# Routing steps at three points of each f-tile, earlier weight requests and a picking mask in halves, in a fused FFT, MLP and capacity-routed MoE kernel

## The chip, the cores and the metric

One core of one Trainium2 chip runs the whole program. The metric is the device time of one execution in microseconds (us). The kernel before took 3361.14 us, the median of three runs from 3357.68 to 3364.51 us.

## The reference, cut to what matters

```python
X = np.fft.fft(np.fft.fft(x, axis=1), axis=2).real      # x: 8 x 3072 x 256
t = X.reshape(24576, 256)
t = (sigmoid(t @ w_gate) * (t @ w_val)) @ w_out         # d_ff 1536
logits = t @ moe2_w_gate                                # 24576 x 8
cap = 24576 // 8                                        # 3072 tokens for each expert
for idx in np.argsort(-logits.flatten()):               # greedy, best pairs first
    tok, e = idx // 8, idx % 8
    if assigned[tok] < 0 and counts[e] < cap:
        assigned[tok] = e; counts[e] += 1
for e in range(8):
    out[assigned == e] = np.maximum(t[assigned == e] @ w1[e], 0) @ w2[e]   # 256 -> 1024 -> 256
```

Every expert ends with exactly 3072 tokens.

## The kernel before, in words

The program has three stages: the transform, the gated MLP, and the routed experts (`Moe2`). The change touches the last alone. There the work goes in eight rounds, one for each expert, in the order in which the experts fill up.

**The experts' matmuls.** A round's 3072 tokens are six token tiles of 512. Each token tile has eight f-tiles (128 of the 1024 hidden columns), so a round has 48 f-tiles. `run` counts them as (c, g) with c from 0 to 11 and g from 0 to 3; two values of c make one token tile. For an f-tile `ffn1` (L1259) issues six matmuls of 512 columns, ScalarE takes the Relu and rounds it (`hh`, L1271), VectorE forms the rest (`hl`, L1272), and `ffn2` (L1275) of the f-tile two places earlier issues twelve matmuls of 256 columns. At the end of a token tile ScalarE copies `y` out and GpSimd (POOL) issues four scatters into `out_dram` (L1293). `xturn` (L1243) transposes the next token tile at g = 2 and 3 of odd c: four transposes on TensorE, `xh` on ScalarE and `xl` on VectorE, with one PSUM buffer for both halves. The expert's weights come by `wload` (L1223), an indirect DMA of POOL, and are split into a high and a low part by `wsplit` (L1232) on ScalarE and VectorE. `gather` (L1211) fetches half a token tile with two indirect DMAs of POOL. POOL executes its queue in the order in which the program issues.

**The routing.** `route(r)` (L1056) finds round r's expert and tokens. If r is above 0 it first takes the best open logit of each token (`best`, eight VectorE instructions over 128x192), marks the winners in V (two VectorE instructions over 128x1536, L1074 and L1076), turns V onto K with twelve transposes in three groups (`turn`, L1020, in PSUM buffers `rt`, of which there are two), and prepares two counts. Then it finds a threshold by 32 bisection steps: two small matmuls onto `cs` (L1095, L1097), two tiny VectorE instructions (`m`, `cand`), a count over one half of K on VectorE (`junk`, L1110) and over the other on ScalarE (`jka`, L1113), whose results the next `cs` matmuls read. Then it finds the expert (`es`, L1121), again takes `best`, scans (L1136), forms the weights' row numbers `wi` (L1140), adds up over partitions with two matmuls on `cs` (L1144, L1145), and writes the ranks RR and RF (L1153 to L1157). The last round has no bisection. `pick(r)` (L1175) turns ranks into token numbers: for each of three h a mask G and a mask H in two halves (VectorE, L1189 and L1192), then four times k two matmuls of H with RF (`rt`, L1201), a small copy on ScalarE (`pc`), two counts on VectorE (`jk`, L1205) and the numbers `idx` (L1207).

**The order.** It is written out when the program is built. `route` and `pick` are generators; each `yield wait, cost` gives the number of beats until the next step and a cost in us. `beat` (L1316) is called once for each f-tile, ahead of `ffn1`. It adds 1.96 us to a budget, less 0.6 for each weight split or transpose of the f-tile, and advances the two streams: the chain of `route` whenever its wait is over, the picks only while the budget is at least 0.2. `want` (L1327) forces steps out at once where a gather or a weight load needs them: the weight loads stand at (10, 1) and (10, 3) of the round before, the next round's first two gathers at (10, 2) and (10, 3), the others 8 f-tiles ahead of their transposes. `chain` (L1298) starts `route(r)` once six of the 24 token columns of round r-1 are picked. Before round 0 all of `route(0)` and the first picks are forced, then four more steps of the chain.

The engines each execute in program order, so a `cs` matmul, a `turn` or a pick's matmul stands in TensorE's queue between the matmuls of the experts, and a count stands in VectorE's queue between the `hl`.

```python
            for c in range(12):
                at = (r, c - 2 - c % 2, c % 2) if c > 1 else (r - 1, 10, 2 + c)
...
                    self.beat(0.6 * len(split))
                    self.ffn1(r, x, 4 * o + g)
                    late.append((r, C, 4 * o + g, self.hid))
                    for p in split:
                        p[0](*p[1:])
                    if len(late) > CFG['lag']:
                        self.ffn2(*late.pop(0))
```

## Time and profile before

| | us |
|---|---|
| median of three runs | 3361.14 |
| the profiled execution, its own time | 3368.34 |
| its span | 3366.6 |
| TensorE matmul busy in the span | 3133.5 (93%) |
| VectorE busy | 2712.7 (81%) |
| ScalarE busy | 1524.2 (45%) |
| POOL busy | 1853.0 (55%) |

The span is 1.7 us shorter than the execution's own time. The stretches of it: the transform to about 418 us, the MLP to about 1994 us, the first routing to 2092 us, then the eight expert rounds, the last of which ends at 3343 us, and the last scatters. Busy time of TensorE counts pipelined matmuls, so that a full engine reads as all of a stretch. An idle time in square brackets is that of the engine just ahead of the instruction, with what ended it.

### The profile page before, as it was taken

Reading aid. Unit: us, or ns where it says so; the run is one execution under the profiler, and the core shown is the slowest. Engines: PE = TensorE matmul, PEld = TensorE weight load, DVE = VectorE, ACT = ScalarE, POOL = GpSimd, SP = SyncE. Lnnn points to the kernel's source line nnn. Section 1 sums busy time; section 2 is a strip of 40 time slices with the busy share of each in tenths; the row PEclk is TensorE's granted clock in tenths of the full one; section 3 lists DMA queues with packets and bytes.
Section 4 is the critical chain, followed back from the end, with each engine's and each line's share of the span. In section 5 each row is a group of like instructions: output and inputs, shape, how many; then the busy total and the mean of one; then the engine's idle time right before and its main releaser. Section 6 shows DMA issues by size and latency. Waiting matters only on the chain.

```text
span 3366.6 us, 62238 instructions
## 1 busy us (share of the span) xinstructions
PE 3133.5 (93%) x23169; PEld 2974.8 (88%) x23169; DVE 2712.7 (81%) x5727; ACT 1524.2 (45%) x2790; POOL 1853.0 (55%) x1821
## 2 busy tenths in 40 slices
PE   5887999999999999999999972999999999999997
PEld 5776999999999999999999972888888888888887
DVE  8998789999989899899999987777777787876432
ACT  4334444544444444444444443535353545453332
POOL 4656677777777777777777741332323332323332
PEclk8999999999999999999999985999999999999999
DMA  5547011111111111111111101111111121211110
GB/s 220 176 156 216 23 27 30 36 30 36 29 38 27 32 34 30 36 30 37 30 36 27 30 14 38 44 62 43 64 41 62 42 64 42 68 44 62 53 61 32
DMA packets 101916, 185.31 MB, mean 55 GB/s; under 512 B 14861, under 2 KB 79462, under 8 KB 96494
## 3 DMA queue, kind: packets, MB, share of 16 engines
q1 hardware_dynamic: 80430, 113.34, 11.4%
q0 software_dynamic: 20736, 67.92, 6.4%
q8 instruction: 183, 3.00, 0.4%
q14 instruction: 119, 0.97, 0.1%
q10 hardware_dynamic: 448, 0.07, 0.0%
HBM read 112.73 MB, written 68.53 MB: 54 GB/s over the span
## 4 chain that ended last, share of the span: by engine, by line
PE 83%; DVE 9%; issue 4%; DMA 2%; ACT 1%; POOL 1%; SPq 0%; POOLq 0%; DVEq 0%; ACTq 0%
PE acc L785 8%; PE acc L786 8%; PE acc L787 8%; PE uv L760 8%; PE uv L761 8%; PE uv L762 8%; PE f L1266 5%; PE f L1287 5%; PE f L1285 5%; PE f L1286 5%; PE f L1267 5%; PE f L1268 5%; DVE tm L1173 1%; PE xt L1253 1%; PE xx L336 1%
## 5 line engine op out<-in xcount | busy, mean ns | idle before, releaser
L906 POOL TENSOR_TENSOR h<-gt,z 128x512 f32<-128x512 f32 x575 | 746.4, 1298 | 418.0 <-ACT gt L921 382.1
L908 ACT CAST hh<-h 128x512 fp32r<-128x512 f32 x576 | 359.5, 624 | 747.0 <-POOL h L906 736.1
L785 PE MATMUL acc<-oh,hh 128*128 128x264 f32 x2304 | 655.9, 285 | 0.0
L786 PE MATMUL acc<-ol,hh 128*128 128x264 f32 x2304 | 655.5, 285 | 0.0
L760 PE MATMUL uv<-pqh,gh 128*128 128x256 f32 x2304 | 646.3, 281 | 9.5 <-DVE z L775 9.5
L787 PE MATMUL acc<-oh,hl 128*128 128x264 f32 x2304 | 654.5, 284 | 0.0
L761 PE MATMUL uv<-pql,gh 128*128 128x256 f32 x2304 | 645.5, 280 | 0.0
L762 PE MATMUL uv<-pqh,gl 128*128 128x256 f32 x2304 | 645.0, 280 | 0.0
L770 DVE SCALAR_TENSOR_TENSOR us<-bc,w,uv 128x256 f32<-128x256 f32 x1152 | 501.7, 477 | 119.8 <-PE uv L762 111.0
L1293 POOL DMA_INDIRECT out_dram<-y,tok x192 | 193.5, 1008 | 711.4 <-ACT y L1290 390.5
L1272 DVE SCALAR_TENSOR_TENSOR hl<-f,hh 128x512 fp32r<-128x512 f32 x384 | 264.9, 690 | 302.2 <-ACT hh L1271 289.5
L917 POOL TENSOR_TENSOR hl<-h,hh 128x320 fp32r<-128x320 f32 x574 | 508.1, 885 | 0.0
L760 PEld LDWEIGHTS uv<-pqh,gh 128*128 128x128 f32 x2304 | 434.9, 189 | 10.5 <-issue 8.5
L1285 PE MATMUL f<-w1h,hh 128*128 128x256 f32 x1536 | 443.1, 288 | 0.0
L1287 PE MATMUL f<-w1h,hl 128*128 128x256 f32 x1536 | 435.8, 284 | 0.0
L761 PEld LDWEIGHTS uv<-pql,gh 128*128 128x128 f32 x2304 | 435.3, 189 | 0.0
L762 PEld LDWEIGHTS uv<-pqh,gl 128*128 128x128 f32 x2304 | 435.1, 189 | 0.0
L1286 PE MATMUL f<-w1l,hh 128*128 128x256 f32 x1536 | 435.0, 283 | 0.0
L786 PEld LDWEIGHTS acc<-ol,hh 128*128 128x128 f32 x2304 | 435.0, 189 | 0.0
L787 PEld LDWEIGHTS acc<-oh,hl 128*128 128x128 f32 x2304 | 434.4, 189 | 0.0
L785 PEld LDWEIGHTS acc<-oh,hh 128*128 128x128 f32 x2304 | 434.1, 188 | 0.0
L774 DVE TENSOR_TENSOR z<-us,uv 128x512 f32<-128x512 f32 x576 | 395.4, 687 | 19.8
(436 smaller groups left out, 6659.5 us busy)
## 6 DMA issues: line engine op xcount, KB each, us to landing
X_d<-x SPq DMA_DIRECT2D x48, 528.0 KB
xt<-in_x_dram SPq DMA_DIRECT2D x24, 1024.0 KB
pq<-PQ_d SPq DMA_DIRECT2D x48, 256.0 KB
bc<-R_d SPq DMA_DIRECT2D x48, 256.0 KB
PQ_d<-po SPq DMA_DIRECT2D x24, 384.0 KB
dw<-in_wgv_dram SPq DMA_DIRECT2D x16, 384.0 KB
PQ_d<-po SPq DMA_DIRECT2D x8, 386.0 KB
dw<-in_moe_w_out_dram SPq DMA_DIRECT2D x8, 384.0 KB
```

Of the source, the lines that this page charges most:

```text
L760: pe.matmul(o, wh, h[:, q], start=True, stop=False)
L761: pe.matmul(o, wh, l[:, q], start=False, stop=False)
L762: pe.matmul(o, wl, h[:, q], start=False, stop=True)
L770: v.scalar_tensor_tensor(us[:, m], bc[:, 1], self.w128[:, m * NF + ft:m * NF + ft + 1], p[:, 0, m * 256:m * 256 + 256], op0=OP.mult, op1=O ...
L785: pe.matmul(o, x, wh, start=(ft == 0), stop=False)
L786: pe.matmul(o, x, wl, start=False, stop=False)
L787: pe.matmul(o, y, wh, start=False, stop=(ft == NF - 1))
L906: (g if n < N else v).tensor_mul(h[m], gt.pop(m), z.pop(m)[:, :, 1])
L917: g.tensor_sub(HL[:, 0:pl], H[:, 0:pl], HH[:, 0:pl])
L1285: pe.matmul(o, hh[:, s], wh[:, f], start=(f == 0 and t % 2 == 0), stop=False)
L1286: pe.matmul(o, hh[:, s], wl[:, f], start=False, stop=False)
L1287: pe.matmul(o, hl[:, s], wh[:, f], start=False, stop=(f == 7 and t % 2 == 1))
```

## The change

The planner is called three times for each f-tile: ahead of `ffn1`, inside it after the fourth matmul, and inside `ffn2` after the first three. A beat adds 0.65 us, and most waits are two or three beats. A bisection step waits two beats, or three when its number is odd. `best` is issued in two halves with a wait between. The weights' row numbers are formed right after `es`, and a weight load wants only these. The second weight load moves from (10, 3) to (10, 2), the first two gathers of the next round from (10, 2) and (10, 3) to (10, 3) and (11, 0). The mask H is issued half by half, ahead of the picks that read it. `route(r)` starts no earlier than round r-1. The four forced steps ahead of round 0 are gone.

```diff
@@ -946,8 +946,8 @@
 NE, CAP, F2 = 8, 3072, 1024
 NT = 192
 BIG = 1.5e38
-CFG = {'NV': 768, 'T': (1, 1, 1, 2, 1), 'cap': 0.2, 'f1': 2, 'f2': 2, 'gate': 6, 'hb': 5, 'hy': 1, 'ky': 1, 'lag': 2, 'lim': 0.2, 'n': 1, 'pre': 2, 'pre2': 2, 'rt': 2, 'v': (1, 1, 2,
-       1), 'w1': (10, 1), 'w2': (10, 3), 'wsub': 'vector', 'xt': 1, 'sp':
+CFG = {'NV': 768, 'cap': 0.2, 'f1': 2, 'gate': 2, 'hb': 5, 'lag': 2, 'lim': 0.2, 'rt': 2, 'w1': (10, 1), 'w2': (10, 2),
+       'wsub': 'vector', 'xt': 1, 'sp':
...
 
@@ -1058,7 +1058,7 @@
         nc, R, ps, L = self.nc, self.R, self.ps, self.L
         v, a, g, pe = nc.vector, nc.scalar, nc.gpsimd, nc.tensor
         last = r == NE - 1
-        T, NV = CFG['T'], CFG['NV']
+        NV = CFG['NV']
         K, V = self.K, self.V
         S_ = R.tile([128, 2, NT], F32, name="S_")
         f2 = R.tile([128, 2, NT], F32, name="f2")
@@ -1068,18 +1068,20 @@
         if not last:
             tm = R.tile([128, NT], F32, name="tm")
             if r > 0:
-                self.best(tm, L, self.open, OP.min)
+                self.best(tm, L, self.open, OP.min, 0)
+                yield 2, 2.2
+                self.best(tm, L, self.open, OP.min, 4)
                 v.tensor_max(tm, tm, self.asg)
-                yield CFG['v'][0], 2.4
+                yield 3, 2.4
                 v.tensor_tensor(V, L, tm[:, :, None].to_broadcast([128, NT, NE]), op=OP.not_equal)
-                yield CFG['v'][1], 1.7
+                yield 2, 1.7
                 v.scalar_tensor_tensor(V, V, -BIG, L, op0=OP.mult, op1=OP.add)
-                yield CFG['v'][2], 1.7
+                yield 3, 1.7
                 for h in range(3):
                     self.turn(ps.tile([128, 512], F32, name="rt", bufs=CFG['rt']), 4 * h, 4)
-                    yield CFG['ky'], 0
+                    yield 1, 0
                 self.odd(R.tile([128, 1536 - NV], I32, name="kk"))
-                yield CFG['v'][3], 1.35
+                yield 2, 1.35
             cand = R.tile([128, 1], I32, name="cand")
             m = R.tile([128, 1], I32, name="m")
             junk = R.tile([128, 1536], BF, name="junk")
@@ -1088,7 +1090,7 @@
             if r > 0:
                 for i in range(2):
                     self.count0(i, 6 * i, 6, junk)
-                yield 1, 1.7
+                yield 3, 1.7
             for b in range(31, -1, -1):
                 p = ps.tile([128, 8], F32, name="cs")
                 both = 0 < b < 31
@@ -1111,7 +1113,7 @@
                     if b > 1:
                         with nc.allow_low_precision(reason="whole numbers up to 1024"):
                             a.activation(jka, self.Ko.bitcast(F32), AF.Sign, bias=thr, scale=-1.0, accum_out=cnt[:, 1:2])
-                yield 1, 0.2 + (b > 0) * n / 960
+                yield 2 + b % 2, 0.2 + (b > 0) * n / 960
             p = ps.tile([128, 512], F32, name="rt", bufs=CFG['rt'])[:, 0:128]
             pe.transpose(p, cand.bitcast(F32).to_broadcast([128, 128]), self.ident)
             tau = R.tile([128, 1], F32, name="tau")
@@ -1119,15 +1121,19 @@
             v.tensor_reduce(tau, t8, axis=AX.X, op=OP.max)
             v.scalar_tensor_tensor(t8, t8, tau, self.rio, op0=OP.is_ge, op1=OP.mult)
             v.tensor_reduce(es, t8, axis=AX.X, op=OP.max)
+            self.rows(r, es)
             v.tensor_scalar(t8, self.rio, es, -BIG, op0=OP.not_equal, op1=OP.mult)
-            yield T[0], 0.5
-            self.best(tm, V, t8, OP.add)
+            yield 1, 0.7
+            self.best(tm, V, t8, OP.add, 0)
+            yield 2, 2.2
+            self.best(tm, V, t8, OP.add, 4)
             v.tensor_scalar(st, tm, tau, None, op0=OP.is_gt)
             v.tensor_scalar(ti, tm, tau, None, op0=OP.is_equal)
-            yield T[1], 2.6
+            yield 3, 2.6
         else:
             v.scalar_tensor_tensor(t8, self.closed, 1.0, self.rio, op0=OP.is_lt, op1=OP.mult)
             v.tensor_reduce(es, t8, axis=AX.X, op=OP.max)
+            self.rows(r, es)
             v.tensor_scalar(st, self.asg, 0.0, None, op0=OP.is_lt)
             v.memset(ti, 0.0)
 
@@ -1135,11 +1141,7 @@
         for i in range(2):
             v.tensor_tensor_scan(S_[:, i], self.ones, f2[:, i], 0.0, op0=OP.mult, op1=OP.add)
         v.tensor_copy(tot, S_[:, :, NT - 1])
-
-        wi = R.tile([128, 1], I32, name="wi", bufs=2)
-        v.scalar_tensor_tensor(wi, self.wm, es, self.wb, op0=OP.mult, op1=OP.add)
-        self.ew[r] = wi
-        yield T[2], 0.8
+        yield 3, 1.3
         p = ps.tile([128, 8], F32, name="cs")
         pe.matmul(p[:, 0:2], self.mats[:, 2], tot, start=True, stop=True)
         pe.matmul(p[:, 2:4], self.mats[:, 3], tot, start=True, stop=True)
@@ -1156,20 +1158,27 @@
         v.tensor_copy(RF[:, 0:193], RR[:, 1:194])
         v.tensor_copy(RF[:, 193:194], RR[:, 193:194])
         self.slots[r] = self.pick(r)
-        yield T[3], 1.0
+        yield 2, 1.0
         if not last:
             v.scalar_tensor_tensor(self.closed, self.rio, es, self.closed, op0=OP.is_equal, op1=OP.add)
             v.tensor_scalar(self.open, self.closed, -2 * BIG, BIG, op0=OP.mult, op1=OP.add)
             v.tensor_sub(tm, RR[:, 1:193], RR[:, 0:192])
             v.tensor_scalar(tm, tm, 2 * BIG, -BIG, op0=OP.mult, op1=OP.add)
             v.tensor_max(self.asg, self.asg, tm)
-            yield T[4], 0.9
-
-    def best(self, out, V, lim, op):
+            yield 1, 0.9
+
+    def rows(self, r, es):
+
+        wi = self.R.tile([128, 1], I32, name="wi", bufs=2)
+        self.nc.vector.scalar_tensor_tensor(wi, self.wm, es, self.wb, op0=OP.mult, op1=OP.add)
+        self.ew[r] = wi
+
+    def best(self, out, V, lim, op, e0):
 
         v = self.nc.vector
-        v.tensor_scalar(out, V[:, :, 0], lim[:, 0:1], None, op0=op)
-        for e in range(1, NE):
+        if e0 == 0:
+            v.tensor_scalar(out, V[:, :, 0], lim[:, 0:1], None, op0=op)
+        for e in range(max(e0, 1), e0 + 4):
             v.scalar_tensor_tensor(out, V[:, :, e], lim[:, e:e + 1], out, op0=op, op1=OP.max)
 
     def pick(self, r):
@@ -1188,11 +1197,12 @@
             H = R.tile([128, 1024], F32R, name="H")
             v.tensor_scalar(G, self.io, se[:, h:h + 1], None, op0=OP.is_ge)
             yield 1, 0.45
-            for i in (0, 512):
-                v.scalar_tensor_tensor(H[:, i:i + 512], self.io[:, i:i + 512], se[:, 3 + h:4 + h], G[:, i:i + 512],
-                                       op0=OP.is_lt, op1=OP.mult)
-                yield CFG['hy'] if i else 1, 0.6
             for k in range(4):
+                if k % 2 == 0:
+                    i = 256 * k
+                    v.scalar_tensor_tensor(H[:, i:i + 512], self.io[:, i:i + 512], se[:, 3 + h:4 + h], G[:, i:i + 512],
+                                           op0=OP.is_lt, op1=OP.mult)
+                    yield 1, 0.6
                 p = ps.tile([128, 2, 256], F32, name="rt", bufs=CFG['rt'])
                 j = 8 * h + 2 * k
                 jk = R.tile([128, 2, NT], BF, name="jk")
@@ -1206,7 +1216,7 @@
                                     op1=OP.add, accum_out=ct[:, j + i:j + i + 1])
                 v.scalar_tensor_tensor(idx[:, s], ct[:, s], 128.0, pc[:, s], op0=OP.mult, op1=OP.add)
                 self.ready[r] = j + 2
-                yield CFG['n'], 0.75
+                yield 2, 0.95
 
     def gather(self, r, c):
 
@@ -1264,6 +1274,8 @@
         s = slice(f * 128, f * 128 + 128)
         for d in range(2):
             pe.matmul(p, wh[:, d, s], xh[:, d], start=(d == 0), stop=False)
+            if d == 1:
+                self.beat(0)
             pe.matmul(p, wh[:, d, s], xl[:, d], start=False, stop=False)
             pe.matmul(p, wl[:, d, s], xh[:, d], start=False, stop=(d == 1))
         hh = R.tile([128, 512], F32R, name="hh", bufs=CFG['hb'])
@@ -1285,6 +1297,8 @@
             pe.matmul(o, hh[:, s], wh[:, f], start=(f == 0 and t % 2 == 0), stop=False)
             pe.matmul(o, hh[:, s], wl[:, f], start=False, stop=False)
             pe.matmul(o, hl[:, s], wh[:, f], start=False, stop=(f == 7 and t % 2 == 1))
+            if t == 0:
+                self.beat(0)
             if f == 7 and t % 2 == 1:
                 y = R.tile([128, 2, D], F32, name="y", bufs=3)
                 nc.scalar.copy(y, self.p2[t // 2])
@@ -1297,7 +1311,7 @@
 
     def chain(self):
         for r in range(self.rounds):
-            while r > 1 and self.ready.get(r - 1, 0) < CFG['gate']:
+            while r > self.round + 1 or (r > 1 and self.ready.get(r - 1, 0) < CFG['gate']):
                 yield 1, 0
             yield from self.route(r)
 
@@ -1315,7 +1329,7 @@
 
     def beat(self, other):
 
-        self.bud = min(max(self.bud, -1.0), CFG['cap']) + 1.96 - other
+        self.bud = min(max(self.bud, -1.0), CFG['cap']) + 0.65 - other
         for i, s in enumerate(self.streams):
             if s[1] is not None:
                 s[1] -= 1
@@ -1326,38 +1340,35 @@
 
     def want(self, r, c=None):
 
-        while r not in self.slots:
+        while r not in (self.ew if c is None else self.slots):
             self.advance(1 if r > 0 and self.ready.get(r - 1, 0) < 24 else 0)
         while c is not None and self.ready.get(r, 0) < 2 * (c + 1):
             self.advance(1)
 
     def run(self):
-        self.ready, self.bud, self.p2 = {}, 0.0, {}
+        self.ready, self.bud, self.p2, self.round = {}, 0.0, {}, 0
         self.streams = [[self.chain(), 1], [self.picks(), 1]]
-        self.want(0, 0)
-        self.wload(0, 0)
-        self.gather(0, 0)
-        self.wload(0, 1)
+        self.want(0)
+        for k in range(2):
+            self.wload(0, k)
+        for c in range(2):
+            self.want(0, c)
+            self.gather(0, c)
         for i in range(4):
             self.wsplit(0, 0, i)
-        for i in range(CFG['pre']):
-            self.advance(0)
-        for i in range(CFG['pre2']):
-            self.advance(0)
-        self.want(0, 1)
-        self.gather(0, 1)
         for h in range(2):
             x = self.xturn(0, 0, h)
         late = []
         plan = {}
         for r in range(self.rounds):
             for c in range(12):
-                at = (r, c - 2 - c % 2, c % 2) if c > 1 else (r - 1, 10, 2 + c)
+                at = (r, c - 2 - c % 2, c % 2) if c > 1 else (r - 1, 10 + c, 3 * (1 - c))
                 plan.setdefault(at, []).append((self.gather, r, c))
             for k in range(2):
                 plan.setdefault((r - 1, *CFG[f'w{k + 1}']), []).append((self.wload, r, k))
         for r in range(self.rounds):
             nxt = r + 1 < self.rounds
+            self.round = r
             for c in range(12):
                 C, o = divmod(c, 2)
                 n = (r, C + 1) if C < 5 else (r + 1, 0) if nxt else None
```

## Rows read from the trace of the kernel before

**Rows 1.** Windows of round 1 and of round 7: length, busy time of each engine, clock.
```profile
2251.40:2414.30 162.90, 154.70 (x1018) 137.60 (x1016) 123.08 (x314) 76.69 (x155) 53.69 (x57) 0.97 0.17 53
3206.90:3343.10 136.20, 135.85 (x889) 123.08 (x888) 41.06 (x62) 41.83 (x73) 40.02 (x45) 1.00 0.13 41
```

**Rows 2.** Waits of TensorE from 2080 us on: total us, times, longest.
```profile
PE xt L1253 <- DMA xg<-X_d,idx: 45.7, 23, 13.2
PE xt L1253 <- DVE xl L1256: 11.5, 8, 1.9
```

**Rows 3.** Timeline ahead of round 0: start, length, engine, line, what [idle before].
```profile
2057.91 4.11 DVE L1173 SCALAR_TENSOR_TENSOR tm<-V,t,tm 128x192 f32<-128x192 f32 x7
...
2064.00 0.16 DVE L1148 COPY o<-cs 128x4 f32<-128x4 f32 x1 [0.17 <-PE cs L1145]
2064.14 1.21 POOL L1225 DMA_INDIRECT w0r<-in_moe_w_dram,wi  x1 [68.66 <-DVE wi L1140]
...
2066.41 1.41 DVE L1192 SCALAR_TENSOR_TENSOR H<-io,se,G 128x512 fp32r<-128x512 f16 x2
...
2068.99 0.16 DVE L1207 SCALAR_TENSOR_TENSOR idx<-ct,pc 128x2 int32<-128x2 f32 x1
...
2081.45 1.76 DVE L1076 SCALAR_TENSOR_TENSOR V<-V,L 128x1536 f32<-128x1536 f32 x1
...
2085.60 0.94 POOL L1219 DMA_INDIRECT xg<-X_d,idx  x1 [0.30 <-issue]
...
2088.47 0.47 PE L1253 MATMUL xt<-ident,xg 128*128 128x128 f32 x1 [0.87 <-DMA xg<-X_d,idx]
...
2092.07 0.68 PE L1266 MATMUL f<-xh,w0h 128*128 128x512 f32 x1
```

**Rows 4.** Timeline of TensorE, round 1, f-tile (9, 3).
```profile
2373.38 0.39 PE L1266 MATMUL f<-xh,w0h 128*128 128x512 f32 x1
...
2376.82 0.66 PE L1253 MATMUL xt<-ident,xg 128*128 128x128 f32 x4 [1.91 <-DVE xl L1256]
...
2379.78 0.77 PE L1266 MATMUL f<-xh,w0h 128*128 128x512 f32 x1
```

**Rows 5.** Timeline, round 2, one f-tile of the bisection.
```profile
2478.43 0.16 PE L1097 MATMUL cs<-cnt,mats 128*128 128x1 f16 x1
...
2480.74 0.69 DVE L1272 SCALAR_TENSOR_TENSOR hl<-f,hh 128x512 fp32r<-128x512 f32 x1 [0.67 <-ACT hh L1271]
...
2481.36 0.17 PE L1097 MATMUL cs<-cnt,mats 128*128 128x1 f16 x1
```

**Rows 6.** Timeline of all engines at the end of round 6.
```profile
3194.22 0.99 POOL L1219 DMA_INDIRECT xg<-X_d,idx  x1 [0.30 <-issue]
...
3195.52 0.96 POOL L1219 DMA_INDIRECT xg<-X_d,idx  x1 [0.30 <-issue]
3195.94 0.68 DVE L1238 TENSOR_TENSOR w0l<-w0r,w0h 128x512 fp32r<-128x512 f32 x1
...
3198.04 0.94 POOL L1219 DMA_INDIRECT xg<-X_d,idx  x1 [0.30 <-issue]
3199.29 0.94 POOL L1225 DMA_INDIRECT w1r<-in_moe_w_dram,wi  x1 [0.30 <-issue]
```

**Rows 7.** Timeline of all engines at the end of round 1.
```profile
2396.96 0.99 POOL L1219 DMA_INDIRECT xg<-X_d,idx  x1 [0.30 <-issue]
...
2402.12 1.75 DVE L1076 SCALAR_TENSOR_TENSOR V<-V,L 128x1536 f32<-128x1536 f32 x1
2402.13 2.56 POOL L1219 DMA_INDIRECT xg<-X_d,idx  x1 [0.30 <-issue]
...
2404.99 0.95 POOL L1225 DMA_INDIRECT w1r<-in_moe_w_dram,wi  x1 [0.30 <-issue]
```

**Rows 8.** Timeline, two bisection steps with nothing beside them.
```profile
2040.30 0.16 DVE L1103 TENSOR_SCALAR m<-cs 128x1 int32<-128x1 f32 x1 [0.32 <-PE cs L1097]
...
2042.10 0.16 DVE L1103 TENSOR_SCALAR m<-cs 128x1 int32<-128x1 f32 x1 [0.32 <-PE cs L1097]
```

## The prediction, made before the change was run

> **What bounds the kernel now.** I read the windows first. The change touches only the expert rounds, and these are bound by TensorE: round 7, beside which no routing runs, takes 136.2 us with TensorE busy for 135.9, and round 1 takes 162.9 with TensorE busy for 154.7 and VectorE for 123.1 against 41.1 [rows 1]. So a round pays some 27 us for the routing of the next, and nothing else there is worth looking at. Then the waits of TensorE from 2080 us on: 45.7 us for gathered tokens, 14.0 of them ahead of round 0 (13.2 and 0.87), the rest once a round in the transposes of (11, 2); and 11.5 us in 8 waits for `xl` [rows 2, 3]. No wait for a count is listed there: with one bisection step for each f-tile the count is always ready. The rest of the 27 us is matmuls that the routing itself issues, and stays. What the change can win lies in those two waits and in the start, where the first expert matmul comes at 2092.07 though the first row number is there at 2068.99 [rows 3].
>
> **The change, part by part.** Sums are against the profiled execution (3368.3 us), which is 0.2% above the median of 3361.1; differences are put on the median.
>
> *Start, gain.* The second gather is late because four chain steps, V among them until 2083.2, stand ahead of its picks on VectorE; it is issued at 2085.60 and its tokens reach TensorE at 2088.47, so 2.87 us from issue to use [rows 3]. Without these steps the second k follows the first by one k (0.95 us, an estimate: four or five of the small operations around 2068.99), and the four gather DMAs go 1.25 us apart (0.94 and the 0.30 ahead of it) from 2069.4: the last is issued near 2073.2 and used near 2076.2. From there to the first f matmul it is 3.6 us, as now [rows 3], plus 1.7 us because the second half of H (0.7) and the matmuls of the third k now stand ahead of it. That gives 2081.5 in place of 2092.1: 10.5 us gained. The weight requests come 6.5 us earlier, but the weights already land before the tokens, so that is worth nothing here.
>
> *Start, given back.* The four steps now lie in the first f-tiles. From 2081.5 on VectorE has to do, up to the end of V: two k (1.9), closing (1.3), `best` (eight operations of 0.59: 4.8 with the last maximum), two passes over V (3.5), G (0.5), four `hl` and two or three weight remainders (0.6 each in a full queue, 4): 17 us, to 2098.5. TensorE reaches `turn` in (0, 1) after four f-tiles and a beat, near 2093.6, and must wait: 5.0 us lost. Together -5.5.
>
> *The forced steps, gain.* With one beat per f-tile `route` needs 47 f-tiles and starts only when six columns of the round before are picked, and `best`, the scans and the sums fall at (9, 2) to (10, 0), on top of the transposes. In round 1 f-tile (9, 3) took 6.40 us; TensorE waited 1.91 for `xl`, and the first matmul after it took 0.77 where 0.39 is usual, which is TensorE at 1.2 instead of 2.4 GHz [rows 4]. An f-tile with a bisection step takes 2.93 [rows 5], with four transposes about 3.4, so 3.0 us too much. Six rounds at that are 18; the waits alone are 11.5 [rows 2]. I take 16. Under the new waits `route` has 18 beats to the first bisection step, 80 for the 32 steps (16 times 2 + 3), and some 15 after it: the expert is known at (8, 0), the first k falls at (9, 1), and the first gather wants it at (10, 3), so nothing is forced any more: -16.
>
> *The wait for tokens at (11, 2).* POOL works through four scatters, each waiting for the one before, and only then issues the gathers; this stays, and so does the wait. Two things change on POOL's queue. The second weight load now stands ahead of the gathers instead of behind: 1.25 us later [rows 6], seven times, +8.8. And V is no longer built there: in round 1 the four gathers took 8.03 us to the weight load, in round 6, which has no `best`, 5.07 [rows 6, 7]; two more rounds are like round 1 and one half so, together 3.5 times 3.0: -10.3. Sum -1.5. The gathers' place in the program, one f-tile later, costs nothing, since POOL is not free before that.
>
> The row says that two passes over V of 1.75 us made a gather take 2.56 [rows 7]; a weight remainder of 0.68 that ran beside a gather left it at 0.96 [rows 6]. The Trainium skill (SBUF — State Buffer, "Who interferes with whom") states that a VectorE instruction with two SBUF inputs contends with a GpSimd instruction that reads SBUF, and whoever comes second is blocked for the whole of it. By that rule the remainders and masks left in (11, 0) and (11, 1) would hold gathers too, up to 0.7 us each, and some 1.4 us of the 3.0 would not come back: the sum would be 5 us higher, by an estimate from it. By the row it is not, and I go by the row.
>
> *The start of a round, loss.* `best` and V used to run under the wait at (11, 2), where VectorE is idle otherwise. Now `route(r)` may not start before round r-1, so they stand at (0, 0) to (0, 2). Up to the end of V VectorE needs 4.8 + 3.5 + two `hl` and two remainders (2.4): 10.9 us from the round's start. TensorE reaches the first `turn`, at the second beat of (0, 3), after 9.4 us: 1.5 us of wait. The second `turn` needs the PSUM buffer of a k whose counts stand behind V: 0.8 more. Five rounds at 2.3: +11.5. Bounds: 0, if the queue drains 15% faster, and 4.
>
> *The bisection, loss.* A step alone takes 1.80 us from `m` to `m` [rows 8]. An f-tile of 2.93 us [rows 5] is cut by columns (6 x 512 and 12 x 256) into 0.98, 0.85 and 1.10, so two beats are 1.83, 2.08 or 1.95: hardly more than the step. In VectorE's queue `hl` starts 2.31 us after the f-tile's start [rows 5] and ends near 3.0. A step at the third beat (1.83) stands behind it, so its `m` comes at 2.9 instead of 2.05, its count at 4.5, and the next `cs`, if two beats later at 3.91, waits 0.57. A step at the second beat delays `hh` and `hl` by its ScalarE half, and so the step after it, which mostly has three beats. Followed through, five f-tiles with six steps lose 0.5 us, a round 2.6, six rounds +16. Bounds: 0, and 8 a round if the transposes, the copies of `y` and late counts add to it.
>
> *The expert's choice, loss.* From the threshold at (8, 0) to the mask at (9, 0) VectorE has `es` and its company (1.6, as six of the small operations between 2064.00 and 2066.41), `best` 4.8, scans 1.7, ranks and G 2.4, closing 1.3 and half of H 0.7 [rows 3]: 12.5 us, with four `hl` between them 14.9, from the first `hl`'s end at 3.0: 17.9. TensorE reaches the sums' matmuls and then the first k after five f-tiles, 14 to 15 us. It waits about 3.0, six rounds: +18. It is the work that was forced before, spread over more f-tiles, but still faster than VectorE can do it. Bounds: 0 and 5 a round.
>
> Masks in halves save 0.7 us once and are counted above. No DMA of SP's queue is moved.
>
> **Sum.** -5.5 - 16 - 1.5 + 11.5 + 16 + 18 = +22.5 us: 3384 on the median, 3391 for the profiled execution.
>
> **The rivals.** *Faster.* VectorE keeps pace: `turn`, the sums and the first k find their operands ready, and a count is there within two beats. For it: VectorE is busy for only 123 of 163 us in a round [rows 1], and TensorE has `hl` buffers for five f-tiles. Against it: these three read VectorE's result directly, no buffer helps. It decides at the three places above, and holds if VectorE's queue is 15 to 20% shorter than I count. Then -5.5 - 16 - 1.5 = -23: 3338. Chance 0.27.
>
> *Slower still.* Each new wait of 1 to 3 us lowers the clock as that of 1.91 us did in round 1 [rows 4], which cost 1.1 us beyond the wait. With three such waits a round and six rounds that is up to 20, with the upper bound of the bisection more: 3405 to 3415. Half the rounds before show such waits without a fall of the clock. Chance 0.15.
>
> *No change.* The spread steps lose just what the forced ones lost. Within 0.2% (6.7 us, about what a measurement of this kernel can tell from no change). That is also the case if the steps fall in the same places as before, which the counted beats exclude. Chance 0.12.
>
> **How the numbers follow.** My forecast, 3370 to 3398, has 0.46. With the rivals: faster 0.27, same 0.12, slower 0.61. The range leaves out a tenth at each end: 3338 to 3408. The forecast's own range is 3370 to 3398.
>
> **What would show it.** Right: the first f matmul near 2081 us; no wait above 1.5 us at (9, 3); new waits of TensorE at `turn` for V (1 to 2 us), at `cs` for `junk` (tens of us in all), at L1144 for `tot` and at the first `rt` of a round for H; the tokens' wait at (11, 2) as long as now, with the weight load ahead of the gathers. Wrong: no wait for a count and rounds of 156 us or less, or rounds that lose over 6 us in the bisection alone.

## The result and the profile after

The changed kernel takes 3403.31 us (median of four runs, 3401.69 to 3406.06) against 3361.89 us (four runs, 3357.68 to 3364.51) for the kernel before on the same chip: a ratio of 1.0125, with a 95% interval from 1.0108 to 1.0143. It is 41.4 us slower. The forecast was 3384, with a range of 3338 to 3408: the direction is right and the range holds the time, but the range of the forecast's own case (3370 to 3398) does not. The profiled execution took 3403.46 us; against that of before (3368.34, which is 6.5 us above the median of its kernel) that is 35.1 us more.

First the windows of round 1 and round 7, which answer to [rows 1].

```profile
2258.30:2424.50 166.20, 156.11 (x1021) 136.37 (x1020) 124.80 (x325) 76.70 (x157) 52.11 (x56) 0.98 0.17 53
3240.90:3378.10 137.20, 137.20 (x889) 123.82 (x888) 41.13 (x62) 41.75 (x73) 39.91 (x45) 1.00 0.13 41
```

Round 1 is 3.3 us longer, with about the same matmuls and work on VectorE. Round 7, beside which no routing runs, is 1.0 us longer too, which no term of the sum foresaw. Then the waits of TensorE from 2080 us on, which answer to [rows 2].

```profile
PE xt L1263 <- DMA xg<-X_d,idx: 29.9, 18, 4.1
PE cs L1097 <- DVE junk L1112: 12.5, 33, 1.6
PE rt L1211 <- DVE H L1203: 12.1, 12, 2.1
PE rt L1025 <- DVE V L1078: 10.4, 6, 3.0
PE cs L1146 <- DVE tot L1143: 7.4, 6, 1.5
```

The wait for `xl` (11.5 us in 8) is gone. Four waits stand in the list that were not in it: for counts, for H, for V and for `tot`, 42.4 us together. The wait for gathered tokens fell ahead of round 0, from 18.7 us to 6.6 if counted from 2060 us on, but not at (11, 2).

The start, which answers to [rows 3]: the first gather, without V ahead of the second gather's pick, and the first expert matmul.

```profile
2070.86 0.95 POOL L1229 DMA_INDIRECT xg<-X_d,idx  x1 [9.49 <-issue]
...
2083.05 0.68 PE L1276 MATMUL f<-xh,w0h 128*128 128x512 f32 x1
```

In f-tile (9, 3) of round 1, where [rows 4] had a wait of 1.91 us and a slow matmul, TensorE goes through, in 3.48 us instead of 6.40:

```profile
2388.53 0.39 PE L1276 MATMUL f<-xh,w0h 128*128 128x512 f32 x1
...
2390.15 0.60 PE L1263 MATMUL xt<-ident,xg 128*128 128x128 f32 x4
...
2392.01 0.39 PE L1276 MATMUL f<-xh,w0h 128*128 128x512 f32 x1
```

Two of the new waits, in round 2: the first transpose of V at (0, 3), and the group sums at (8, 3).

```profile
2433.92 1.76 DVE L1078 SCALAR_TENSOR_TENSOR V<-V,L 128x1536 f32<-128x1536 f32 x1
...
2435.73 0.66 PE L1025 MATMUL rt<-ident,V 128*128 128x128 f32 x4 [1.48 <-DVE V L1078]
...
2541.98 0.17 DVE L1143 CAST tot<-S__30924 128x2 f16<-128x2 f32 x1
...
2542.21 0.16 PE L1146 MATMUL cs<-tot,mats 128*128 128x2 f16 x1 [1.47 <-DVE tot L1143]
```

In both TensorE is released as soon as VectorE's instruction is done. The granted clock (the third number from the end of a line) in four stretches tells whether such waits also slow the matmuls behind them: (0, 3) of round 2; (8, 3) and (9, 0) of round 2; behind the wait for tokens at (11, 2) of round 1; and behind the wait for V at (1, 0) of round 0.

```profile
2433.10:2439.00 5.90, 4.42 (x33) 3.75 (x32) 5.18 (x10) 1.83 (x4) 2.11 (x2) 1.00 0.13 46
2538.80:2548.10 9.30, 6.46 (x43) 5.59 (x42) 8.59 (x26) 1.20 (x2) 4.12 (x5) 1.00 0.15 46
2415.30:2422.10 6.80, 5.86 (x22) 4.87 (x22) 1.35 (x2) 0.59 (x1) 3.39 (x6) 0.50 0.23 64
2101.40:2104.70 3.30, 3.30 (x16) 3.20 (x16) 0.98 (x3) 1.15 (x3) 0.00 (x0) 0.50 0.02 5
```

After waits of 1.5 us it stays at 1.00 (2.4 GHz). In the expert rounds it falls to 0.50 (1.2 GHz) only at the waits for tokens, as before, and at the one of 3.0 us in round 0. In the kernel before it had also fallen at the forced steps of rounds 0 to 2 (0.50 from 2377.6 to 2381.0 us in round 1), and not at those of rounds 3 to 5, though the waits of rounds 1 to 5 there are all 1.8 to 1.9 us.

The next table takes the f-tiles of both profiled executions, each from its first matmul to that of the next (the last f-tile of all is left out), and adds them up by the terms of the forecast.

| stretch | before | after | difference | forecast |
|---|---|---|---|---|
| first f matmul at | 2092.1 | 2083.1 | -9.0 | -10.5 |
| round 0, (0, 0) to (1, 3): `turn` | 23.9 | 31.5 | +7.6 | +5.0 |
| (9, 2) to (10, 0), rounds 0 to 5: forced steps | 73.6 | 60.7 | -12.9 | -16 |
| (11, 2), rounds 0 to 6: tokens | 71.5 | 69.4 | -2.1 | -1.5 |
| rounds 1 to 5, (0, 0) to (1, 3): start of a round | 128.5 | 136.8 | +8.3 | +11.5 |
| rounds 1 to 5, (2, 0) to (8, 0): bisection | 392.3 | 406.3 | +14.0 | +13.4 |
| round 0, (2, 0) to (8, 0): bisection | 78.7 | 88.4 | +9.7 | +2.6 |
| (8, 1) to (9, 1), rounds 0 to 5: expert's choice | 87.7 | 104.0 | +16.3 | +18 |
| all other f-tiles | 394.7 | 397.9 | +3.2 | 0 |
| sum | | | +35.1 | +22.5 |

### The profile page after: what moved, and what is told of

Its sections match the earlier page's. It is cut to its first block, busy times and chain, and to the rows that moved or that the text cites. A ratio compares the mean times of both kernels' runs of the same rounds, so it can differ in the third digit from the quotient of the medians.

```text
span 3401.6 us, 62319 instructions
## 1 busy us (share of the span) xinstructions
PE 3152.4 (93%) x23169; PEld 2971.7 (87%) x23169; DVE 2707.7 (80%) x5727; ACT 1522.1 (45%) x2790; POOL 1844.8 (54%) x1821
## 4 chain that ended last, share of the span: by engine, by line
PE 72%; DVE 18%; ACT 3%; issue 3%; DMA 3%; POOL 1%; SPq 0%; POOLq 0%; ACTq 0%; DVEq 0%; another core or an unknown queue 0%
PE acc L785 8%; PE acc L786 8%; PE acc L787 8%; PE uv L760 8%; PE uv L761 8%; PE uv L762 8%; PE f L1279 3%; PE f L1297 3%; PE f L1276 3%; PE f L1280 3%; PE f L1298 3%; PE f L1299 3%; DVE hl L1284 2%; DVE junk L1112 2%; DVE tm L1182 2%
## 5 line engine op out<-in xcount | busy, mean ns | idle before, releaser
L1297 PE MATMUL f<-w1h,hh 128*128 128x256 f32 x1536 | 452.3, 294 | 1.9 <-ACT y L1304 1.9
```

The costliest lines, as they stand in the source:

```text
L1297: pe.matmul(o, hh[:, s], wh[:, f], start=(f == 0 and t % 2 == 0), stop=False)
```

## The experiments

**The addresses.** Since the weights are asked for ahead of the scans, their tiles are also reserved earlier and lie elsewhere. The first three kernels move tiles and no instruction. Here and below a ratio is to the kernel before on the same chip, whose median lay between 3358.55 and 3366.24 us on the chips used, so kernels are compared by their ratios.

```diff
@@ e1_old_addresses: the changed kernel, tiles reserved in the old order @@
+        if r == 0:
+            R.tile([128, 2], F16, name="tot")
...
@@ e2_new_addresses: the kernel before, tiles reserved in the new order @@
@@ e3_pad_64: the changed kernel @@
+        if r == 0:
+            self.R.tile([128, 16], F32, name="pad")
```

> The changed kernel, every instruction as it is, with the tiles that stay from round to round reserved in the order of the kernel before, so that each lies at the address that it has there (w0h at 71744 instead of 64128, xg at 104512 instead of 145472). The sum of the prediction has no term for the f-tiles without any routing, and these take 2.83 us after against 2.78 before: 0.05 us in each of 384 f-tiles is some 17 to 19 us of the 41. Theory P (the addresses of the weights set the pitch of the wide matmuls): the median pitch goes from 234 back to 227 ns and the time falls by 15 to 20 us, to 3383 to 3388. Theory S (the pitch comes with the new order of instructions): the pitch stays at 234 and the time at 3403 plus or minus 4.

> The kernel before, every instruction as it is, with its tiles reserved at the addresses of the changed kernel. Theory P: the median pitch of the wide matmuls goes from 227 to 234 ns and the time rises by 15 to 20 us, to 3377 to 3382. Theory S: 227 ns and 3362 plus or minus 4.

> The changed kernel with one unused tile of 64 bytes ahead of the weights, so that w0h lies at 64192 instead of 64128, and all weights after it 64 bytes higher too. Theory P64 (what counts in an address is its remainder by 128, which was 64 before and is 0 after): 227 ns and 3383 to 3388, as with the old addresses. Theory PB (it is where the weights lie against other tiles, some thousands of bytes off): 234 ns and 3403, although the old addresses help. Theory S: 3403 too, and the old addresses do not help.

Measured: 3401.39, 3361.78 and 3406.00 us, at ratios of 1.0122 (1.0106 to 1.0137), 1.0005 (0.9996 to 1.0014) and 1.0137 (1.0121 to 1.0152). Round 7 of e1 and of e2:

```profile
3239.00:3374.30 135.30, 135.30 (x888) 123.17 (x888) 41.05 (x62) 41.80 (x73) 40.01 (x45) 1.00 0.13 40
```

```profile
3199.30:3336.50 137.20, 137.20 (x889) 123.65 (x888) 41.10 (x62) 41.79 (x73) 40.05 (x45) 1.00 0.13 40
```

All three are as Theory S expected, and Theory P falls as a cause of the loss: the addresses do move the pitch of the wide matmuls (from `xl` to `xh` its median is 234 ns in the changed kernel, 229 in e1; 227 in the kernel before, 233 in e2), and a round that TensorE fills alone follows, 135.3 against 137.2, but the whole kernel moves by less than 2 us. In the rounds with routing the f-tiles keep their length (round 3 takes 165.7 us in the changed kernel and in e1). Another 64 bytes do not help. So what was lost came with the order of the instructions.

**The tokens' wait.**

```diff
@@ e4_gathers_early, against the changed kernel @@
-                at = (r, c - 2 - c % 2, c % 2) if c > 1 else (r - 1, 10 + c, 3 * (1 - c))
+                at = (r, c - 2 - c % 2, c % 2) if c > 1 else (r - 1, 9 + c, 3 * (1 - c))
@@ e11_w2_behind, against the changed kernel @@
-       'w2': (10, 2)
+       'w2': (11, 1)
```

> The changed kernel with the next round's first four gathers three and two f-tiles earlier (c = 0 ahead of f-tile (9,3), c = 1 ahead of (10,0), instead of (10,3) and (11,0)), so that GpSimd issues them before the four scatters of block 4 and both weight loads. Theory G (the wait of the transposes at (11,2) for the gathered rows is GpSimd's order, four scatters of 2.7 us each ahead of the gathers): (11,2) falls from 9.8 us to 4 to 5 in seven rounds, 35 to 40 us less, 3363 to 3368. Rival (what ends the wait next is late as well: VectorE's picks for the indices, or the first weights that now come after four gathers): half of that or less, 3383 to 3403, with a wait for the indices on GpSimd at (9,3) or one for w0h at (0,0) in the trace.

> The changed kernel (late gathers, as it was given) with the second weight load asked for at (11,1), behind the first four gathers on GpSimd, instead of at (10,2), ahead of them. The sum of the prediction had +8.8 for that load standing ahead of the gathers (1.25 us of issue in seven rounds). Theory G (the wait of the transposes at (11,2) is GpSimd's order): (11,2) falls by 1 to 1.5 us in seven rounds, 7 to 10 us less than the changed kernel, a ratio to the kernel before of 1.009 to 1.010. Rival L (the second weights now land too late for their split at (0,0)): VectorE and ScalarE wait for w1r, no gain or a loss, 1.012 or more.

e4 took 3364.59 us, a ratio of 1.0017 (1.0008 to 1.0026). POOL at the end of round 1 in e4, and the transposes of (11, 2) there:

```profile
2378.46 1.00 POOL L1229 DMA_INDIRECT xg<-X_d,idx  x1 [3.36 <-PE rt L1211]
...
2382.28 0.95 POOL L1229 DMA_INDIRECT xg<-X_d,idx  x1 [0.30 <-issue]
...
2394.03 1.28 POOL L1307 DMA_INDIRECT out_dram<-y,tok  x1 [9.54 <-ACT y L1304]
...
2407.28 0.60 PE L1263 MATMUL xt<-ident,xg 128*128 128x128 f32 x4
```

The gathers are out 11 us before the first scatter, and the transposes wait for nothing. (11, 2) fell from 69.4 to 22.9 us in seven rounds. Of these 46.5 us about 30 are the waits themselves (29.9 for tokens, by the list of TensorE's waits above); the rest goes with the clock, which no longer falls behind them. In e4 it stays at 1.00 to the end of round 7:

```profile
2110.00:3340.00 1230.00, 1183.35 (x7804) 1039.60 (x7803) 832.97 (x2110) 540.75 (x1087) 394.93 (x430) 1.00 0.17 53
```

Of the gain 6.3 us were lost again at (9, 2) to (10, 0), where ScalarE's copy `pc` starts 1.8 us after its pick's matmul instead of 0.4 and `xl` is late behind it. Theory G holds: the wait at (11, 2) is POOL's order.

e11 took 3393.56 us, a ratio of 1.0102 (1.0087 to 1.0117). At the end of round 6, the changed kernel has the weight load `w1r` ahead of the gathers, e11 behind them:

```profile
3226.80 0.99 POOL L1235 DMA_INDIRECT w1r<-in_moe_w_dram,wi  x1 [0.30 <-issue]
3228.09 0.96 POOL L1229 DMA_INDIRECT xg<-X_d,idx  x1 [0.30 <-issue]
```

```profile
3218.25 0.99 POOL L1229 DMA_INDIRECT xg<-X_d,idx  x1 [0.30 <-issue]
...
3223.31 0.94 POOL L1235 DMA_INDIRECT w1r<-in_moe_w_dram,wi  x1 [0.30 <-issue]
```

(11, 2) takes 59.1 us instead of 69.4 in seven rounds: -10.3, where the forecast had priced the load's place at 8.8. The second weights are not late: (0, 0) to (1, 3) of rounds 1 to 5 takes 136.8 us in both. This part of the change, the weight load put ahead of the gathers, cost about what was worked out.

**The three new waits.** All kernels from here on stand on e4, with the route of round 1 left as it is unless said.

```diff
@@ e5_turn_later: after V @@
-                yield 3, 1.7
+                yield 5 if r > 1 else 3, 1.7
@@ e6_bits_3 @@
-                yield 2 + b % 2, 0.2 + (b > 0) * n / 960
+                yield 3 if r > 1 else 2 + b % 2, 0.2 + (b > 0) * n / 960
...
+                self.round = r + (c >= 10)
@@ e7_sums_later @@
-        yield 3, 1.3
+        yield 5 if r > 1 else 3, 1.3
...
-                    yield 1, 0.6
+                    yield 2 if r > 1 else 1, 0.6
...
-                at = (r, c - 2 - c % 2, c % 2) if c > 1 else (r - 1, 9 + c, 3 * (1 - c))
+                at = (r, c - 2 - c % 2, c % 2) if c > 1 else (r - 1, 10, c)
@@ e8_all_later: all of these @@
```

> The kernel with early gathers (e4_gathers_early), and from the route of round 2 on the transposes of V two points of an f-tile later (5 beats after V instead of 3). Theory W (the start of a round costs what TensorE waits for V, because the step is asked for before VectorE has done it): the five waits of 1.5 us at the first transpose of V go, 7 to 9 us less than e4, 3355 to 3358. Rival M (VectorE does its work in order, so that the same lateness shows at the next step): the time of e4, 3365 plus or minus 3, with longer waits for the first counts.

> e4 with, from the route of round 2 on, every bisection step three points after the last (instead of two and three in turn), for which the route begins eight f-tiles earlier, at (10,0) of the round before. Theory W (the bisection costs what TensorE waits for the counts at the steps that have only two points): of the 11.8 us that e4 waits there, the 8 to 10 of these five rounds go, 3353 to 3358. Rival M (the first steps of the route now lie beside the picks, the split of the weights and the gathers at the end of a round, and VectorE is late there): 3365 or more, with the waits for V and H longer than in e4 (10.3 and 17.6 us).

> e4 with, from the route of round 2 on, the group sums five points after the scans instead of three and each pair of picks two points after its half of the mask instead of one; the first gathers at (10,0) and (10,1), still ahead of the scatters. Theory W: the waits for tot (1.3 to 1.5 us in five rounds) and for H (1.3 to 2 us in five) go, 12 to 16 us less than e4, 3349 to 3353. Rival M (the lateness moves to the next step, or the gathers wait for indices that come later): 3360 to 3367.

> e4 with the edits of e5_turn_later, e6_bits_3 and e7_sums_later together. Theory W: the three savings add up, 27 to 35 us less than e4, 3330 to 3338. Rival M: no better than the best of the three alone.

| kernel | median us | ratio to before | 95% interval |
|---|---|---|---|
| e5_turn_later | 3378.57 | 1.0036 | 1.0024 to 1.0049 |
| e6_bits_3 | 3375.97 | 1.0026 | 1.0015 to 1.0036 |
| e7_sums_later | 3348.16 | 0.9944 | 0.9927 to 0.9960 |
| e8_all_later | 3353.26 | 0.9963 | 0.9949 to 0.9977 |

The kernel before took 3366.24 us beside these four; e4 stands at 1.0017. **e7** is Theory W, and beats both kernels: by the ratios it is 24 us below e4, more than the 12 to 16 expected. Two of its waits of TensorE:

```profile
PE rt L1211 <- DVE H L1203: 7.5, 11, 2.2
...
PE cs L1146 <- DVE tot L1143: 0.6, 1, 0.6
```

The wait for `tot` is left in round 0 alone, and (8, 1) to (9, 1) takes 90.0 us in rounds 0 to 5 against 104.0 in the changed kernel: 14.0 of the 16.3 us that the expert's choice had cost are back. The 6.3 us that e4 had lost at (9, 2) to (10, 0) are back too (67.0 in e4, 60.7 in e7); whether the later picks or the later gathers did that was not taken apart. The start of the rounds and the bisection of rounds 1 to 5 took 5.6 us more than in e4.

**e5** is Rival M. The waits for V that its edit aimed at are gone, and the time rose. F-tile (0, 3) of round 2 in e5:

```profile
2423.97 1.76 DVE L1078 SCALAR_TENSOR_TENSOR V<-V,L 128x1536 f32<-128x1536 f32 x1
2426.85 0.74 DVE L1203 SCALAR_TENSOR_TENSOR H<-io,se,G 128x512 fp32r<-128x512 f16 x1
2427.65 0.74 PE L1211 MATMUL rt<-RF,H 128*128 128x194 f32 x2 [3.86 <-DVE H L1203]
```

The two points left free were taken by a pick of the round under way. Its H stands behind V on VectorE, and TensorE waits 3.86 us for it, ahead of the transposes. Behind that wait the granted clock is at 0.50 (from 2427.0 to 2433.8 us), and it falls so at the start of rounds 2 to 5: part of e5's loss is matmuls at 1.2 GHz.

**e6** removed what it meant to, but is Rival M in time. In (2, 0) to (8, 0) of rounds 1 to 5 the waits for counts fell from 7.8 us in the changed kernel to 0.3, and the stretch takes 397.8 us, against 405.4 in e4: half of the 14.0 us of the bisection are back, though waits for `xl` of 7.8 us appeared there. And (10, 1) to (11, 1), where the route now begins, rose from 106.0 to 123.1 us, and TensorE waits as long for V as before (these lines are of all rounds and stretches):

```profile
PE rt L1025 <- DVE V L1078: 10.7, 6, 3.0
PE cs L1097 <- DVE junk L1112: 10.4, 16, 1.5
PE f L1279 <- DVE xl L1266: 9.3, 16, 1.2
```

**e8** is Rival M: not the sum of three savings, and no better than e7 alone.

**Who stands behind whom on VectorE.**

```diff
@@ e9_no_picks_behind_v, against e7 @@
+                self.hold = r > 1
...
-                yield 3, 1.7
+                yield 5 if r > 1 else 3, 1.7
...
+                self.hold = False
                 self.odd(R.tile([128, 1536 - NV], I32, name="kk"))
...
-                while s[1] is not None and s[1] <= 0 and (i == 0 or self.bud >= CFG['lim']):
+                while s[1] is not None and s[1] <= 0 and (i == 0 or (self.bud >= CFG['lim'] and not self.hold)):
@@ e10_round0_too, against e9 @@
-                yield 5 if r > 1 else 3, 1.7
+                yield 5, 1.7
...
-                    yield 2 if r > 1 else 1, 0.6
+                    yield 1 if r == 1 else 2, 0.6
@@ e12_split_on_gpsimd, against e7 @@
-       'wsub': 'vector'
+       'wsub': 'gpsimd'
```

> The kernel with later sums (e7_sums_later), and from round 2 on the transposes of V two points later as in e5_turn_later, but with no pick laid between the first step of V and its last transpose. In e5 the wait for V went (10.3 to 3.0 us) and one for H rose (17.6 to 28.9 us), in the f-tile (0,3) that took 9.4 us instead of 5.8. Theory Q (a pick asked for while VectorE still has V's instructions ahead of it takes over the wait, since VectorE works in order): with no pick there (0,3) and (1,0) together take 6 to 7 us instead of 8.7 in five rounds, 8 to 12 us less than e7, whose ratio to the kernel before was 0.9944: 0.991 to 0.992. Rival R (what waits is any next step, so the first counts of the bisection or the later picks take the wait): 0.994 to 0.997.

> e9 with two more edits in round 0 alone: the transposes of V two points later there too, and the picks of round 0 two points after their half of the mask. In round 0 the changed kernel's f-tiles (2,0) to (8,0) took 88.4 us against 78.7 before, with the same picks and steps in them, and the largest idle times in them stand ahead of a pick (1.3 us) and of bisection steps beside picks (1.3, 1.1 us); (0,1,0) took 8.5 us, 3.0 of it a wait for V. Theory Q: some 3 us of the wait for V and 1 to 2 of the picks' go, 3 to 6 us less than e9. Rival R: the same time as e9, within 2 us.

> e7_sums_later with the subtraction of the weight splits (eight of 0.68 us a round, at (11,0) to (11,2) and (0,0) to (1,0)) on GpSimd instead of VectorE. e9 and e10 showed a wait for VectorE moving from V to the counts with its work put off. Theory C (the joint of two rounds is bound by VectorE's work): 5.4 us less work on VectorE a round takes away the wait for V (1.5 us in five rounds, 3.0 in round 0) and part of the picks', 8 to 15 us less than e7, a ratio of 0.990 to 0.992. Rival P (GpSimd's subtraction is slow, or it holds up the gathers and scatters in GpSimd's queue, so that the weights or the rows come late): 0.995 or more, with waits for w0l, w1l or xg.

e9 took 3345.50 us, 0.9962 (0.9949 to 0.9975), and e10 3346.63, 0.9966 (0.9952 to 0.9979): faster than the kernel before, not told apart from e7 or from each other. Both times are Rival R's, but each theory has a part. The start of the rounds behaved as Theory Q says: (0, 0) to (1, 3) fell by 13.0 us in rounds 1 to 5, from 140.6 to 127.6, though part of that is the picks themselves, two or three a round, which have left the stretch. And (2, 0) to (8, 0) rose by 16.2, from 407.8 to 424.0, where the picks put off, 18 in the five rounds, now lie beside bisection steps. TensorE's waits for V fell from 10.4 us in e7 to 3.3, and those for counts rose from 13.5 to 19.6. (2, 3) of round 2 in e9:

```profile
2443.21 0.16 PE L1099 MATMUL cs<-cnt,mats 128*128 128x1 f16 x1
...
2443.74 0.69 DVE L1286 SCALAR_TENSOR_TENSOR hl<-f,hh 128x512 fp32r<-128x512 f32 x1 [0.58 <-ACT pc L1215]
2444.34 0.41 DVE L1217 TENSOR_SCALAR_CACHE_REDUCE jk<-rt,num 128x192 bf16<-128x192 f32 x1
...
2445.21 0.15 DVE L1107 TENSOR_SCALAR m<-cs 128x1 int32<-128x1 f32 x1
...
2446.66 0.16 PE L1099 MATMUL cs<-cnt,mats 128*128 128x1 f16 x1 [1.37 <-DVE junk L1114]
```

The sums are there by 2443.5, but `m` starts at 2445.21, behind an `hl` and the pick's two counts, and the next step waits 1.37 us. In e10 round 0's first eight f-tiles fell by 2.2 us and (2, 0) to (8, 0) by 1.6, but a pick for round 1 at (10, 3), one point after its mask, now waits for H, which stands behind an `hl`:

```profile
2233.74 0.62 PE L1213 MATMUL rt<-RF,H 128*128 128x194 f32 x2 [2.58 <-DVE H L1205]
```

e12 took 3381.55 us, 1.0071 (1.0058 to 1.0083), so Rival P, but with another mechanism than it named. The end of (11, 1) and the start of (11, 2) of round 1 in e12:

```profile
2405.78 5.20 DVE L1217 SCALAR_TENSOR_TENSOR idx<-ct,pc 128x2 int32<-128x2 f32 x1
2405.96 4.99 POOL L1248 TENSOR_TENSOR w0l<-w0r,w0h 128x512 fp32r<-128x512 f32 x4
...
2410.90 0.68 DVE L1284 SCALAR_TENSOR_TENSOR hl<-f,hh 128x512 fp32r<-128x512 f32 x1
2411.63 0.50 PE L1276 MATMUL f<-xh,w0h 128*128 128x512 f32 x1 [1.73 <-DVE hl L1284]
```

A VectorE instruction of 0.16 us took 5.20, as long as the four subtractions on POOL, and what stood behind it was late: (11, 2) and (11, 3) took 75.6 us in seven rounds against 51.8 in e7, and (0, 0) to (1, 3), where the rest of the weights is split, 150.0 us in rounds 1 to 5 against 140.6.

## Why the prediction was right in direction and short in size

The time lies 5 us inside the upper end of the whole range and 5 us above the forecast's own. The mechanism, steps that TensorE reads before VectorE is done, was right at each place where it was priced; several sizes were not.

**The start.** The first f matmul came at 2083.1 for 2081.5: 9.0 us gained of 10.5. From the first pick's matmul (2067.22 before, 2068.16 after) to the first f matmul it is 24.9 us before and 14.9 after: the change gained 10.0 us, and the two executions differ by 0.9 the other way ahead of it. The wait at `turn` in round 0 was foreseen at 5.0. By the forecast's own items it is 3.9: they add up to 16.0 us, not 17. Measured, it is 3.0, with 0.9 for `hl` just ahead of it; the eight f-tiles there cost 7.6, and behind the wait the clock was at 0.50 (2101.4 to 2104.7 us), which the forecast had only in a rival.

**The forced steps.** (9, 3) and (10, 0) fell by 14.5 us in rounds 0 to 5, for the forecast's -16; (9, 2) beside them rose by 1.6, where a pick now stands that was not there before.

**Start of a round, bisection in rounds 1 to 5, expert's choice.** +8.3, +14.0 and +16.3 for +11.5, +13.4 and +18. In the choice 13.7 us are the waits for `tot` and H, and e7, which undid them, gave back 14.0 of the 16.3. In the bisection of rounds 1 to 5 the waits for counts are 7.8 us of the 14.0, and e6, which undid them, gave back half; where the rest of the loss lies is not shown. At the start of a round the waits for V are 7.4 of the 8.3. The second `turn` behind a late pick, for which the forecast had 0.8 a round, shows no wait. The forecast's items for VectorE there add up to 10.7 us, not 10.9, which makes 10.5 for the five rounds. e5 took the waits for V away and lost more to H; in e9 the stretch got shorter by more than the 8.3, but its picks left it too.

**The step that failed first: the bisection of round 0.** The forecast wrote 2.6 us for each of "six rounds". Rounds 1 to 5 lost 2.8 each, but round 0 lost 9.7, above the forecast's bound of 8 a round and above the 6 us that it had named as a sign of being wrong. Two things are different in round 0. First its own picks: seven of them, k5 to k11, stand between its bisection steps, at (1, 3) to (4, 1), while from round 2 on none does. The steps of the changed kernel come at 2 or 3 points whether or not a pick's counts stand ahead on VectorE, as at (3, 3), where the sums before are there at 2139.7 and `m` comes at 2141.87:

```profile
2141.00 0.41 DVE L1215 TENSOR_SCALAR_CACHE_REDUCE jk<-rt,num 128x192 bf16<-128x192 f32 x1
...
2141.87 0.15 DVE L1105 TENSOR_SCALAR m<-cs 128x1 int32<-128x1 f32 x1
...
2143.32 0.16 PE L1097 MATMUL cs<-cnt,mats 128*128 128x1 f16 x1 [1.17 <-DVE junk L1112]
```

From (2, 0) to (4, 2) round 0 lost 6.0 us, the other rounds 1.0 each. Second, its bisection begins two f-tiles later, at (1, 3) and not at (1, 1), so that its last steps reach (8, 0). One of them waits 1.62 us there, behind an `hl` and the `xl` of a transpose, not behind a pick:

```profile
2198.81 0.68 DVE L1266 TENSOR_TENSOR xl<-xt,xh 128x512 fp32r<-128x512 f32 x1
...
2200.86 0.16 PE L1097 MATMUL cs<-cnt,mats 128*128 128x1 f16 x1 [1.62 <-DVE junk L1112]
```

(8, 0) lost 1.8 us in round 0 and nothing in the others. Of the 9.7 us, waits of TensorE for counts are 4.4 in 6 and one for H 1.2; the rest does not show as a wait. No run undid the picks' part as a whole: e10, which put round 0's picks later behind their mask, gave back 1.6. But e9 shows the same price from the other side: 18 picks laid beside bisection steps cost 16.2 us, 0.9 each, and in the changed kernel (2, 0) to (4, 2) takes 41.0 us in round 0, with six picks, and 35.5 in round 2, with none, again 0.9 each. In the kernel before, five picks stood there in round 0 and it took 35.0. This term is 7.1 us of the 12.6 between forecast and profile; 4.1 more are the start and round 0's `turn`, 3.1 the forced steps and 3.2 the other f-tiles, and the start of a round and the expert's choice, overpriced, take 4.9 back.

**The step that failed second: the credit at (11, 2).** -10.3 for V that no longer stretches gathers was taken from the profiled execution, in which V met a gather for 1.95 or 2.56 us in four rounds. e2 is the kernel before but for addresses; its profiled execution ran 6.6 us shorter in the span, V met a gather for so long in two rounds only, and (11, 2) took 63.5 us in seven rounds against 71.5. In rounds 1 to 5 of both executions together, (11, 2) takes 11.6 us in the four rounds in which V stretched two gathers to 1.95 and 2.56 us, 9.9 or 10.0 in the two in which it stretched one to 1.95, and 7.0 to 8.3 in the four others. The changed kernel takes 9.7 or 9.8 in each. So the credit was read from an execution with much of this, and that the term came out (-2.1 for -1.5) on that same execution is luck: against e2 it is +5.9. That fits the 6.3 us by which 41.4 on the medians exceeds 35.1, as far as two executions tell; whether chance or the addresses decide which gather V meets is not shown. The other half of that term, +8.8 for the weight load, was 10.3 by e11.

**The row and the rule on gathers.** By the row that the forecast chose, a remainder `w0l` left a gather at 0.96 us. In the changed kernel a gather that starts beside `w0l` takes 1.43 us and one that starts beside H 1.17 to 1.22, in rounds 0 to 5, 0.7 us a round above 0.95:

```profile
2576.17 0.68 DVE L1248 TENSOR_TENSOR w0l<-w0r,w0h 128x512 fp32r<-128x512 f32 x1
2576.25 1.43 POOL L1229 DMA_INDIRECT xg<-X_d,idx  x1 [0.30 <-issue]
...
2577.99 0.95 POOL L1229 DMA_INDIRECT xg<-X_d,idx  x1 [0.30 <-issue]
```

So the row that the forecast chose was a gather that had started before the remainder. The trace of before held the other case as well, in round 1, between the first two of [rows 7]:

```profile
2398.05 1.28 DVE L1238 TENSOR_TENSOR w0l<-w0r,w0h 128x512 fp32r<-128x512 f32 x2
2398.26 1.31 POOL L1219 DMA_INDIRECT xg<-X_d,idx  x1 [0.30 <-issue]
```

The Trainium skill (SBUF — State Buffer, "Who interferes with whom") says that a VectorE instruction with two SBUF inputs contends with a GpSimd one that reads SBUF, and that the order of issue decides which of them is blocked; the rows of the gathers agree, since the one that starts 0.08 us behind a remainder is held and the one that starts ahead of it is not. e12 agrees that the two contend: there VectorE was the one that waited, 5.20 us for 0.16. Its row starts 0.18 us ahead of the first subtraction's, so the order is not shown by it. By the forecast's estimate from that rule the sum was to be 5 us higher; the gathers show 0.7 in each of six rounds, 4.2.

**The rivals.** *Faster* needed VectorE to keep pace at three places: it does at none. *Slower still* came nearest the time (3403 against 3405 to 3415), but its main cause is not there: the clock stays at 1.00 through the new waits of rounds 1 to 5 and falls only at the one for V in round 0. Its other part, the upper bound of the bisection, held in round 0 alone. *No change* is excluded by the interval.

**What stays open.** Why `pc` starts late in e4. The part of the bisection's loss that shows as no wait: some 6 us in rounds 1 to 5 and 4 in round 0. The 3.2 us in the other f-tiles: 1.0 of it is round 7, where e1 shows the addresses at work; the rest was not taken apart. Nor was it tried to finish all picks of a round before its successor's V begins, which e5 and e9 point to.

## What to carry to other kernels

A step that TensorE reads directly costs nothing only if its producer is done when TensorE gets there, and on an engine that works in order this is decided by what was issued ahead of it, not by the engine's mean load: VectorE was busy for three quarters of a round, and each of the three points asked for early waited. Putting a wait off helped in e7. It only moved the loss where the planner filled the gap with work for the same engine (e5), or where what was put off landed beside other steps for it (e9). Look at each in-order queue for what can go first because it is ready first: four gathers put ahead of four scatters (1.0125 to 1.0017) were worth more than the best placing of small steps tried here (1.0017 to 0.9944). And a wait of TensorE can cost more than its length: the waits at (11, 2) were 30 us, and without them and the fall of the clock behind them 46.5 us came back.

## What the runs showed of the hardware

- In e12 a VectorE instruction with two inputs in SBUF was held for a whole run of GpSimd subtractions (0.16 us became 5.20 while four of them ran 4.99), while `hl`, which reads one input from PSUM, stayed at 0.69 us beside them.
- A gather that GpSimd issued 0.08 us behind the start of a VectorE subtraction of 0.68 us took 1.43 us instead of 0.95; one that had started ahead of it stayed at 0.96.
- The pitch of back-to-back 512-column matmuls changed with where tiles lie in SBUF, 229 against 234 ns in two kernels with the same instructions (e1 and the changed one). It showed where TensorE waits for little else, 135.3 against 137.2 us for 47 f-tiles of round 7, and not in round 3 beside the routing (165.7 in both).
- The granted clock stayed at 1.00 behind TensorE's waits of 1.5 us and fell to 0.50 behind one of 3.0 us and those for tokens of 3 to 4 us. Behind the waits of 1.8 to 1.9 us of the kernel before it fell in two rounds and stayed in three. In e4, which from 2110 us on has none above 1.5 us, it stayed at 1.00 for 1230 us.
- A GpSimd subtraction of 128x512 took 1.25 to 1.32 us in 59 of 60 cases (e12), one on VectorE 0.68.
